# A causal convolution followed by a two-layer product with quick GELU: taps and block sums of the convolution on ScalarE and GpSimd in place of VectorE

## The chip, the cores and the metric

The kernel runs on one core of a Trainium2 chip. A core has TensorE (matmuls, PE in the profile, with PEld for its weight loads), VectorE (DVE), ScalarE (ACT), GpSimd (POOL) and SyncE (SP), which here issues transfers. Each works through its own queue in order, and semaphores tie them together. The metric is the device time of one execution in microseconds (us), the median of the runs.

## The reference, cut to what matters

```python
# x: (8, 4096, 192), weight: (8, 7), w_in: (192, 2048), w_out: (2048, 192)
w = softmax(weight, axis=-1)                 # 8 heads of 24 channels, 7 taps each
x_pad = concatenate([zeros((B, 6, D)), x], axis=1)
y[b, s, h, g] = sum_k w[h, k] * x_pad[b, s + k, h, g]
h = y.reshape(B * S, D) @ w_in
g = h * (1.0 / (1.0 + exp(-1.702 * h)))
return g @ w_out                             # (32768, 192), float32
```

So every token is a weighted sum of itself and the six tokens before it, channel by channel; then come a product to 2048 features, a gating function and a product back to 192 channels. All of it is float32.

## The kernel before, in words

**Tiling.** The 32768 tokens are worked off in 32 steps (`big`) of 1024 tokens: two batches `n` of 512, each as two tiles `o` of 256. The 192 channels are NC = 3 chunks of 64. A convolved chunk lies with both tiles over 128 partitions (64 channels of one tile, 64 of the other) and two blocks of 256 columns (the two batches), so one operation of the convolution has the shape 128 x 512.

**Fewer products.** Both products use a scheme of the Strassen kind. For the first one the six convolved blocks C11 to C32 are joined into V1 to V8 by eight sums (`SUMS_C`, lines 145 to 154), and each of 21 terms (`TERMS`) is one block or sum times one block or sum of `w_in`. For the second, blocks of the gated features are subtracted from one another (`sum_1` to `sum_4`, line 512) and multiplied by blocks of `w_out`.

**A step.** `hidden` (line 531) runs twice in a step, v = 0 and v = 1, with 21 terms each on TensorE (line 492). Four PSUM tiles of two banks, `x`, `y`, `z` and `sums`, are filled, emptied by ScalarE (copies to k15, k16, k18, k19, k20 at lines 543, 549, 557, 559, 565; gating at line 509) or joined by VectorE (lines 554, 562, 566, 574, 575, 587), and filled again. Then `output` (line 649) runs five rounds of the second product (line 597, with line 614), adds their parts (lines 671 to 708), transposes them (line 632) and stores them.

**The preparation of a later step.** `prepare(big)` (line 466) yields small pieces of work for step `big`: three transposes of input (line 414), the taps of the convolution (`conv`, lines 424 to 433), the eight sums (`sums_c`, line 435) and the transfers that bring blocks across the two halves of the partitions (`cross`, line 438). A tap is one operation on VectorE: tap 0 multiplies (line 429), taps 1 to 6 multiply and add to what is there (line 431). The chunks go in the order 0, 2, then the first sum V1 with its transfer, then chunk 1 and the other seven sums.

**What sets the order.** The schedule is written by hand: instructions stand in each engine's queue in the order in which the program makes them. `work(us)` (line 716) takes pieces from the list `todo` as long as their noted cost fits into the given allowance (0.76 for a tap, 0.48 for tap 0, 0.38 for a sum, 0.7 for a transpose); `need(label)` takes all up to a label. The pieces for step `big + 2` are put on the list when the hidden passes of `big` are done, and are taken at the `work` calls in `output` of `big` and in the two `hidden` passes of `big + 1`:

```python
gelu(B11, 0, v, x)                                   # v = 0 and 1
...
act.copy(k16, sums)
last()
if v:
    work(3.2)
pe(y, 6, 14, first=True)
vec.tensor_sub(x, z, k15)
work(2.6)
pe(sums, 13)
act.copy(k19, sums)
```

Further calls are `work(1.1)` after line 566, `work(2.3)` before line 574, and `work(1.2)` and `work(0.7)` around the last two terms. In `output` they are 3.0, 0.7, 0.7 and 4.0. In the queue of the engine that does it, a piece stands exactly where its `work` call is. Buffers bind as well: TensorE may write a PSUM tile again only when ScalarE or VectorE has read it, and k16 shares its memory with u1 and u2 of `output`.

The first step (`first_step`) prepares its own blocks on several engines, and `prepare(1)` runs within it.

Of the kernel before, what the change touches and what calls it, by code (L numbers as in the profile page):

```python
# [8 lines left out]
F32 = mybir.dt.float32  # L9
# [6 lines left out]
def kernel(  # L16
# [29 lines left out]
    nc = tc.nc  # L46
# [5 lines left out]
    P = 128  # L52
# [5 lines left out]
    T = 256  # L58
# [17 lines left out]
    consts = ctx.enter_context(tc.tile_pool(name="consts", bufs=1))  # L76
# [6 lines left out]
    vec, act = nc.vector, nc.scalar  # L83
# [44 lines left out]
    def half(b, u, cols, small):  # L128
# [16 lines left out]
    SUMS_C = [  # L145
        (V1, C31, "-", C11),
        (V2, V1, "-", C32),
        (V3, C12, "+", V2),
        (V4, C22, "+", V2),
        (V5, C21, "-", V4),  # L150
        (V6, C11, "-", V5),
        (V7, C22, "-", C21),
        (V8, C32, "-", C22),
    ]

    def place(big, b):

        if b == V1:
            return V8 if big % 2 else C31
        return C31 if b == V8 and big % 2 else b  # L160

    def own(big):
        return conv_t[:, big % 2 * 2, :, :]
# [169 lines left out]
        dst = w_in_s[:, NC * i : NC * (i + 1), :]  # L333
        round_piece(i, [(lambda v: v.rearrange("p (k f) -> p k f", k=NC), dst)])

    def add_up(v, dst, a, op, b):
        if op == "+":
            vec.tensor_add(v(dst), v(a), v(b))
        elif op == "-":
            vec.tensor_sub(v(dst), v(a), v(b))  # L340
        elif op == "n":
            vec.scalar_tensor_tensor(
                out=v(dst), in0=v(a), scalar=-1.0, in1=v(b), op0=ALU.mult, op1=ALU.subtract
            )
        else:
            vec.tensor_scalar_mul(v(dst), v(a), -1.0)

    def sums_w_in(i):
        add_up(lambda j: w_in_s[:, j, :], *SUMS_W[i])
# [60 lines left out]
    def transpose_x(big, c, n=None):  # L410
# [7 lines left out]
        if c == NC - 1 and n is None:  # L418
            xins.pop(big)

    def conv_src(big, c, k, ns=slice(0, 2)):
        return xts[big][:, c, ns, Q - PAD + k : Q - PAD + k + T]

    def conv(big, c, k, ns=slice(0, 2)):
        src = conv_src(big, c, k, ns)
        dst = own(big)[:, 2 * c + ns.start : 2 * c + ns.stop, :]
        tap = cw[:, c, k : k + 1]
        if k == 0:
            vec.tensor_scalar_mul(dst, src, tap)
        else:  # L430
            vec.scalar_tensor_tensor(  # L431
                out=dst, in0=src, scalar=tap, in1=dst, op0=ALU.mult, op1=ALU.add
            )

    def sums_c(big, i):
        add_up(lambda j: own(big)[:, place(big, j), :], *SUMS_C[i])

    def cross(big, b0, b1):
        for o in range(2):
# [26 lines left out]
    def prepare(big):  # L466

        for c in range(NC):
            yield "", 0.7, lambda c=c: transpose_x(big, c)
        if big + 1 < N_BIG:  # L470
            yield "", 0.0, lambda: load_x(big + 1)

        v1 = place(big, V1)
        for c in (0, 2):
            for k in range(K):
                yield "", 0.76 if k else 0.48, lambda c=c, k=k: conv(big, c, k)
        yield "", 0.38, lambda: sums_c(big, 0)
        yield f"first {big}", 0.0, lambda: cross_when(True, big, v1, v1 + 1)
        for k in range(K):
            yield "", 0.76 if k else 0.48, lambda k=k: conv(big, 1, k)  # L480
        yield "", 0.0, lambda: cross_when(False, big, 0, C31)
        for i in range(1, len(SUMS_C)):
            yield "", 0.38, lambda i=i: sums_c(big, i)
        rest = (C31, V8) if big % 2 else (C31 + 1, NB)
        yield f"all {big}", 0.0, lambda: cross_when(False, big, *rest)
# [235 lines left out]
    def need(label):  # L721
# [9 lines left out]
        op=ALU.mult,  # L731
# [20 lines left out]
    def first_step(fetch):  # L752
# [6 lines left out]
        for k in range(5):  # L759
            conv(0, 0, k, first)  # L760
# [174 lines left out]
```

## Time and profile before

| | before |
|---|---|
| time, median of 2 runs | 2352.9 us (2352.79 to 2353.01) |
| span of the profiled execution | 2351.6 us |
| mean granted TensorE clock | 0.999 |
| ScalarE's gating from SBUF (line 509) | 310 of 1058 ns |
| ScalarE's gating from PSUM (line 509) | 167 of 1016 ns and 35 of 1022 ns |
| VectorE's subtractions of gated blocks, 128 x 2048 (line 512) | 124 of 2284, 62 of 2292, 62 of 2262 ns |
| GpSimd | 23 instructions, 5.8 us busy |
| crossing transfers of V1 (64 KB each) | 1.9 us to landing |

A busy share is an average over the span; whether an engine holds up another is read from the waits and from the order of time. In a group's row the columns are the line, engine, operation, tiles written and read with their shapes, the count, then busy time and the mean ns of one, then the engine's idle time before these operations and who ended it. In a list of waits a row says which engine waited at which line for whom: total us, times, longest.

### The profile page before, as it was taken

How to read it: one execution, taken by the hardware profiler on the slowest of the kernel's cores; microseconds unless marked ns; L12 is line 12 of the kernel's file. 1: busy time of each engine (PE TensorE's matmuls, PEld its weight loads, DVE VectorE, ACT ScalarE, POOL GpSimd, SP SyncE). 2: the span in 40 equal slices, each digit the busy share in tenths (PEclk: the TensorE clock that was granted, in tenths of full speed). 3: DMA queues.
4: the chain of work that ended last, by engine and by line, in shares of the span. 5: the costliest groups of instructions: out<-in, count | busy, mean ns of one | idle time of the engine just before them, and what ended most of it. 6: DMA issues, size and time to landing. Idle time of an engine off the chain costs nothing.

```text
span 2351.6 us, 39193 instructions
## 1 busy us (share of the span) xinstructions
PE 2343.7 (100%) x16856; PEld 892.0 (38%) x16856; DVE 1951.7 (83%) x2186; ACT 1018.4 (43%) x1159; POOL 5.8 (0%) x23
## 2 busy tenths in 40 slices
PE   9999999999999999999999999999999999999998
PEld 5533333333333333333333333333333333333333
DVE  8988888888888888888888888888888888888866
ACT  7234543345533355433454334543345533345433
POOL 0000000000000000000000000000000000000000
PEclk9999999999999999999999999999999999999999
DMA  8323313323123232132331332312323223231010
GB/s 182 69 48 76 68 21 64 63 57 68 36 49 66 55 69 50 35 65 55 68 64 22 68 64 58 68 30 54 67 55 69 46 39 67 55 68 43 17 41 15
DMA packets 197484, 133.67 MB, mean 57 GB/s; under 512 B 108592, under 2 KB 187824, under 8 KB 193344
## 3 DMA queue, kind: packets, MB, share of 16 engines
q1 hardware_dynamic: 196448, 130.92, 27.5%
q8 instruction: 132, 2.16, 0.4%
q14 instruction: 40, 0.33, 0.0%
q10 hardware_dynamic: 832, 0.20, 0.0%
q0 software_dynamic: 32, 0.07, 0.0%
HBM read 53.15 MB, written 25.17 MB: 33 GB/s over the span
## 4 chain that ended last, share of the span: by engine, by line
PE 67%; issue 32%; DMA 0%; DVE 0%; POOL 0%; POOLq 0%; DVEq 0%
PE slot L492 24%; PE slot L597 22%; PE sums L492 11%; PE sums L597 9%; PE slot L614 1%; PE slot L740 0%; PE sums L390 0%; DMA conv_t<-conv_t 0%; DVE xt L414 0%; PE slot L401 0%; POOLq L930 0%; POOL xin L94 0%; PE slot L390 0%; POOL osbs masks.py:199 0%; POOL osbs masks.py:197 0%
## 5 line engine op out<-in xcount | busy, mean ns | idle before, releaser
L492 PE MATMUL slot<-conv_t,w_in_s 64*128 64x512 f32 x3740 | 851.8, 590 | 0.0
L597 PE MATMUL slot<-g,w_out_s 128*32 128x512 f32 (+2 forms) x6864 | 788.7, 568 | 0.0
L492 PEld LDWEIGHTS slot<-conv_t,w_in_s 64*128 64x128 f32 x3740 | 359.6, 187 | 446.8 <-issue 394.6
L431 DVE SCALAR_TENSOR_TENSOR conv_t<-xt,cw,conv_t 128x512 f32<-128x512 f32 (+1 forms) x576 | 424.8, 738 | 13.0
L597 PEld LDWEIGHTS slot<-g,w_out_s 128*32 128x32 f32 x6864 | 241.8, 110 | 455.9 <-issue 439.0
L492 PE MATMUL sums<-conv_t,w_in_s 64*128 64x512 f32 x1660 | 405.4, 592 | 0.0
L509 ACT ACTIVATE g<-room 128x1024 f32<-128x1024 f32 x310 | 321.1, 1058 | 97.5 <-DVE room L574 58.3
L597 PE MATMUL sums<-g,w_out_s 128*32 128x512 f32 (+1 forms) x2304 | 335.0, 587 | 0.0
L512 DVE TENSOR_TENSOR g<-g 128x2048 f32<-128x2048 f32 (+1 forms) x126 | 283.2, 2267 | 4.7 <-PE sums L597 2.4
L492 PEld LDWEIGHTS sums<-conv_t,w_in_s 64*128 64x128 f32 x1660 | 158.3, 187 | 202.9 <-issue 160.9
L509 ACT ACTIVATE g<-slot 128x1024 f32<-128x1024 f32 x167 | 169.4, 1016 | 88.7 <-PE slot L492 88.7
L597 PEld LDWEIGHTS sums<-g,w_out_s 128*32 128x32 f32 x2304 | 93.1, 110 | 152.7 <-issue 146.3
L512 DVE TENSOR_TENSOR room<-g 128x2048 f32<-128x2048 f32 (+1 forms) x64 | 144.6, 2259 | 4.3
L512 DVE TENSOR_TENSOR g<-room,g 128x2048 f32<-128x2048 f32 (+1 forms) x64 | 140.2, 2229 | 0.0
L685 ACT COPY osbs<-slot 32x512 f32<-32x512 f32 (+1 forms) x32 | 18.3, 572 | 251.6 <-PE slot L614 251.6
L597 PE MATMUL slot<-room,w_out_s 128*32 128x512 f32 (+1 forms) x816 | 112.9, 567 | 0.0
L597 PE MATMUL sums<-room,w_out_s 128*32 128x512 f32 x768 | 112.7, 592 | 0.0
L686 DVE TENSOR_TENSOR room<-room,slot 96x512 f32<-96x512 f32 (+1 forms) x32 | 21.6, 675 | 91.1 <-ACT osbs L685 91.1
L670 ACT COPY osbs<-slot 32x512 f32<-32x512 f32 (+1 forms) x32 | 18.4, 574 | 174.4 <-PE slot L597 174.4
L554 DVE TENSOR_TENSOR slot<-slot,room 128x1024 f32<-128x1024 f32 x62 | 75.4, 1216 | 10.8 <-ACT g L509 10.8
L566 DVE TENSOR_TENSOR room<-slot,room 128x1024 f32<-128x1024 f32 x62 | 75.9, 1225 | 6.8 <-DVE room L562 0.5
L574 DVE TENSOR_TENSOR room<-room,sums 128x1024 f32<-128x1024 f32 x31 | 37.8, 1221 | 48.4 <-PE sums L492 48.4
(151 smaller groups left out, 1522.1 us busy)
## 6 DMA issues: line engine op xcount, KB each, us to landing
xin<-in_x_dram SPq DMA_DIRECT2D x240, 180.0 KB, 5.6
conv_t<-conv_t SPq DMA_DIRECT2D x62, 512.0 KB, 4.5
out_dram<-osbs SPq DMA_DIRECT2D x180, 128.0 KB, 2.5
conv_t<-conv_t SPq DMA_DIRECT2D x62, 256.0 KB, 3.6
conv_t<-conv_t SPq DMA_DIRECT2D x62, 64.0 KB, 1.9
xin<-in_x_dram SPq DMA_DIRECT2D x16, 160.0 KB, 5.5
osbs<-in_moe_w_out_dram SPq DMA_DIRECT2D x2, 768.0 KB, 8.8
out_dram<-osbs SPq DMA_DIRECT2D x20, 64.0 KB, 1.8
```

The costliest lines, as they stand in the source:

```text
L431: vec.scalar_tensor_tensor(out=dst, in0=src, scalar=tap, in1=dst, op0=ALU.mult, op1=ALU.add)
L492: nc.tensor.matmul(slot[:, h, :], w_in_s[halves[h], a, v * P : (v + 1) * P], src, start=first, stop=True, skip_group_check=True,)
L509: act.activation(g[:, b, u, v, :, :], src, AF.Gelu_apprx_sigmoid)
L512: vec.tensor_sub(*(half(x, u, cols, small) for x in (dst, a, b)))
L554: vec.tensor_sub(x, z, k15)
L566: vec.tensor_sub(k19, z, k19)
L574: vec.tensor_add(k20, k20, sums)
L597: nc.tensor.matmul(dst[l * Q : (l + 1) * Q, :], w_out_s[:, a, j, c * Q : (c + 1) * Q], half(b, u, cols, small)[:, v, h, :], start=(first a ...
L614: nc.tensor.matmul(dst[l], w_out_s[:, a, j, c * Q : (c + 1) * Q], half(b, u, cols, small)[:, v, h, :], start=(i == 0), stop=(i == NK // 4 ...
L670: act.copy(chunk(v3, 1), blocks(p3c))
L685: act.copy(chunk(v4, 0), blocks(p4c))
L686: vec.tensor_add(v1, v2, p5)
```

## The change

From step 2 on the convolution leaves VectorE. Tap 0 is a multiplication on ScalarE straight into the block. Each of the taps 1 to 6 becomes two operations: ScalarE multiplies into one of six scratch tiles (`taps`, used in turn), and GpSimd adds the scratch to the block. The eight sums of blocks become additions and subtractions on GpSimd. Steps 0 and 1 are as before. Its purpose is to take load off VectorE and give it to the two engines that have less to do. The `work` calls and the noted costs of the pieces stay as they are.

```diff
-    def add_up(v, dst, a, op, b):
+    def add_up(v, dst, a, op, b, eng=vec):
         if op == "+":
-            vec.tensor_add(v(dst), v(a), v(b))
+            eng.tensor_add(v(dst), v(a), v(b))
         elif op == "-":
-            vec.tensor_sub(v(dst), v(a), v(b))
+            eng.tensor_sub(v(dst), v(a), v(b))
...
+    NT = 6
+    taps = consts.tile([P, NT, 2, T], F32)
+    turn_of = [0]
...
         tap = cw[:, c, k : k + 1]
-        if k == 0:
+        if big > 1:
+            if k == 0:
+                act.mul(dst, src, tap)
+                return
+            tmp = taps[:, turn_of[0] % NT, :, :]
+            turn_of[0] += 1
+            act.mul(tmp, src, tap)
+            nc.gpsimd.tensor_add(dst, dst, tmp)
+        elif k == 0:
             vec.tensor_scalar_mul(dst, src, tap)
         else:
             vec.scalar_tensor_tensor(
...
     def sums_c(big, i):
-        add_up(lambda j: own(big)[:, place(big, j), :], *SUMS_C[i])
+        add_up(
+            lambda j: own(big)[:, place(big, j), :],
+            *SUMS_C[i],
+            eng=nc.gpsimd if big > 1 else vec,
+        )
```

## The prediction

> **What bounds the kernel now.** I read the page's busy line first, then the chain of work that ended last, then the list of waits, and last the order of ScalarE's work in one steady step.
>
> ```profile
> PE 2343.7 (100%) x16856; PEld 892.0 (38%) x16856; DVE 1951.7 (83%) x2186; ACT 1018.4 (43%) x1159; POOL 5.8 (0%) x23
> ...
> PE 67%; issue 32%; DMA 0%; DVE 0%; POOL 0%; POOLq 0%; DVEq 0%
> ```
>
> A busy PE need not be a PE at its rate, so I checked the rate. The chain in order of time has runs of 64 matmuls of L597 in 6.87 us (0.1073 each) and of 36 of L492 in 7.72 us (0.2144 each). Multiplied by the counts: 5400 x 0.2144 = 1158; 10352 matmuls of 512 columns on L597 and L614 x 0.1073 = 1111; 784 of 256 columns at half of that = 42; 128 of 128 columns about 4; L740 10.4. Sum 2325 us. Of the 2351.6 us span only 27 us (1.1%) isn't TensorE at its steady rate. VectorE's 83% stands beside this and not on it, and the chain has 0% DVE.
>
> The waits show how near ScalarE is:
>
> ```profile
> PEld sums L492 <- ACT room L549: 13.1, 31, 0.8
> ...
> PEld slot L492 <- ACT g L509: 7.9, 32, 0.6
> ...
> PEld slot L492 <- ACT room L557: 7.3, 31, 0.2
> ...
> PEld slot L492 <- ACT room L543: 4.5, 16, 0.3
> ```
>
> In nearly every step TensorE comes to these PSUM tiles just as ScalarE has emptied them. Waits of 0.1 to 0.4 us are still swallowed by the matmuls in flight; there is little beyond that. Here is ScalarE in a steady step (start, duration, work, idle before):
>
> ```profile
> 611.46 1.01 ACT L549 COPY room<-slot 128x1024 f32<-128x1024 f32 x1 [0.99 <-DVE osbs L632]
> 613.73 1.01 ACT L557 COPY room<-slot 128x1024 f32<-128x1024 f32 x1 [1.26 <-PE slot L492]
> ...
> 618.09 1.01 ACT L565 COPY room<-slot 128x1024 f32<-128x1024 f32 x1
> 618.98 2.02 ACT L509 ACTIVATE g<-room 128x1024 f32<-128x1024 f32 x2
> 621.92 1.06 ACT L509 ACTIVATE g<-room 128x1024 f32<-128x1024 f32 x1 [0.93 <-DVE room L574]
> 622.89 1.00 ACT L509 ACTIVATE g<-slot 128x1024 f32<-128x1024 f32 x1
> 623.79 1.02 ACT L582 COPY sums<-slot 128x1024 f32<-128x1024 f32 x1
> 624.73 1.05 ACT L509 ACTIVATE g<-room 128x1024 f32<-128x1024 f32 x1
> 626.66 1.01 ACT L543 COPY room<-sums 128x1024 f32<-128x1024 f32 x1 [0.88 <-PE sums L492]
> ...
> 631.76 1.01 ACT L557 COPY room<-sums 128x1024 f32<-128x1024 f32 x1 [0.55 <-PE sums L492]
> ```
>
> The 43% is an average. In the two hidden passes of this step (606.55 to 642.6 us, 42 terms of 4 matmuls, 0.858 us each) ScalarE has 26 operations at about 0.95 us from start to start: 24.7 of 36.0 us. It rests in the output products that follow.
>
> **What the Trainium skill says.** *ScalarE: Activation LUTs*, "What ACT_TABLE_LOAD costs": an ACTIVATE with one pointer operand takes 280 ns + 0.833 ns per element, and neighbours overlap by 93 ns; for 512 that is 707 ns, 614 from start to start. The trace agrees (below). *GPSIMD Engine Reference*, section 3.1: a float32 two-input add of 2048 elements takes 4497 ns on GpSimd, 1.96 times VectorE's. The trace has only one of 64 elements. *SBUF — State Buffer*, "SBUF: two separate sides": GpSimd and VectorE share a port pair as an exclusive lock, against VectorE operations with two SBUF inputs or in a two-port mode; the loser waits for the whole instruction. No row of before shows this, since GpSimd does nothing then.
>
> **The change part by part.** The rows that price it:
>
> ```profile
> L431 DVE SCALAR_TENSOR_TENSOR conv_t<-xt,cw,conv_t 128x512 f32<-128x512 f32 x558 | 416.1, 746 | 12.4
> L340 DVE TENSOR_TENSOR conv_t<-conv_t 128x256 f32<-128x256 f32 x186 | 73.2, 421 | 3.2
> L429 DVE TENSOR_SCALAR conv_t<-xt,cw 128x512 f32<-128x512 f32 x93 | 43.6, 468 | 0.0
> L734 ACT ACTIVATE g<-room,cw 128x64 f32<-128x64 f32 x7 | 1.8, 334 | 0.8 <-DVE cw L408 0.8
> L274 POOL TENSOR_TENSOR room<-osbs 128x64 f32<-128x64 f32 x1 | 0.3, 307 | 0.0
> ```
>
> *Removed from VectorE*, per step: 18 x 0.746 + 3 x 0.468 + 8 x 0.42 = 18.2 us of its 60 us. It was hidden behind TensorE, so worth nothing by itself. One thing is returned: in the first pass L549 waits for L632, the last turn of VectorE's output work, because k16 and u1, u2 are one buffer. With no taps ahead of it that turn ends about 0.9 us sooner, and L549 starts when TensorE's term ends, at 611.2 and not 611.46.
>
> *Added to GpSimd*: between 307 ns at 64 and 4497 at 2048 lie 2.11 ns per element, so an add of 512 is estimated at 1.25 us, a sum of 256 at 0.71; 18 x 1.25 + 8 x 0.71 = 28.2 us of a 72.45 us step (the same run of matmuls returns every second step, at 570.43 and 715.31 us in the chain). Who waits for it: the crossing DMA of V1, and ScalarE when it reuses one of six scratch tiles. V1 comes out about 19 us into the hidden passes and is wanted by TensorE after 32; the other sums end about 37 us in and are wanted at 72. The longest run of scratch writes is 4, and each add six back is done by then. All hidden. Lock: VectorE's L512 work (8 x 2.28 = 18.2 us a step) stands in the output part, where only two adds of GpSimd fall; the subtractions are wanted 1.9 us or more after they end, so one add of 1.25 us is hidden.
>
> *Added to ScalarE*: 21 multiplications a step. L734 shows 7 of 64 elements in 1.78 us: 0.332 us each, 0.24 from start to start. L309 (768 elements, pointer bias) takes 0.936 and its kind starts 0.84 apart. Linear between: at 512, 0.72 us, and 0.62 from start to start. That is 13.0 us a step, 8.1 of it (13 of 21) in the hidden passes: 24.7 + 8.1 = 32.8 of 36.0. They fit on average, but the queue is in order and `work` puts them in bunches ahead of operations that empty PSUM. The order of the changed program shows: 3 ahead of L557, 1 ahead of the two gelus at 618.98 and 3 behind them, 2 ahead of L543 of the second pass, 4 ahead of its L557. The other 8 lie in the output part, where ScalarE is idle for 4 to 8 us at a time: nothing. On the trace's times:
>
> 1. First L557: L549 at 611.20, free at 612.12, three multiplications to 613.98, copy done at 614.99. TensorE wants it at term 10, 615.13. Holds by 0.14: 0.
> 2. L565 at 618.09, free 618.99; one multiplication, two gelus (619.61, 620.57), three multiplications from 621.53; gelu of k20 at 623.39 and of x at 624.36, done at 625.37. The second pass begins by writing that slot at 606.55 + 21 x 0.858 = 624.57. With 0.08 us from ScalarE's end to TensorE: **0.9 us**.
> 3. Copy at 625.26, gelu at 626.20, two multiplications from 627.16, L543 at 628.40, done 629.41. TensorE, already 0.9 late, has done its term and x's two by 628.88 and must add to that tile: **0.6 us**.
> 4. L549 at 630.71 and last pass's gelu at 631.61, four multiplications from 632.57, L557 at 635.06, done 636.07. TensorE is at that tile by 634.64: **1.5 us**.
>
> After that the step has no multiplications up to the output part, and ScalarE catches up. Sum 3.0 us a step; blocks 2 to 31 are made this way, in 30 steps: 90 us. 2352.9 + 90 = 2443.
>
> Ends: without any overlap of neighbours (0.72) the nine multiplications of items 2 to 4 add 0.9 us and item 1 gives about 0.2: 4.1 a step, 2476. If each of the three waits is 0.3 us shorter (matmuls in flight swallow as much in the waits above): 2.1 a step, 2416.
>
> **The rivals.** *ScalarE's slack hides it, no change.* For it: 43% busy, 3.2 us left in the hidden passes by the sum above. Then 2353, and since only 27 us aren't TensorE at its rate, 2326 is the floor, so faster by 2% (2306) is out. Against: the bunches stand where the waits list shows the least room. Part of it, under 1.5 us a step, ends below 2400. Chance 0.14.
> *GpSimd or its lock adds to it, slower still.* For it: adds of 512 aren't in the trace. Against: 28.2 us and VectorE's 19.6 us with two SBUF inputs leave 25 us of the step; adds would have to take over 2.3 us to fill it. If the lock also held VectorE's PSUM reads (L554, L562, L574), one add's 1.25 us would fall on the path in each step: 30 x 4.25 = 128, 2480. With adds at 3 us, GpSimd's 67 us and VectorE's 19.6 exceed the step by 14 us: 2352.9 + 30 x 14 = over 2770. Chances 0.16 and 0.04.
> *ScalarE's bunches delay TensorE*, the forecast: 0.66, near 2443.
>
> **How the numbers follow.** Below 2400 lies the first rival (0.14, of which 0.01 is faster by 2%, kept for an error in the rate); above 2490 some of the second and its extreme (0.08). Between are 0.78. 2% is 2400, so slower by over 2% has 0.85, within 2% 0.14.
>
> **What would show it.** Right: waits of TensorE for L509, L543's and L557's lines of about 1.0, 0.6 and 1.5 us, each some 30 times; steps of 75.5 us; VectorE near 60%, ScalarE near 60%, GpSimd near 36%; the chain passing through ScalarE. Wrong: TensorE still without waits; ScalarE idle waiting for GpSimd (ring of scratch); VectorE's operations stretched beside adds; or an add far from 1.25 us.

## The result and the profile after

The changed kernel takes 2444.5 us (2443.61 to 2445.39) against 2352.9 us: ratio 1.0388, interval 1.0358 to 1.0418. It is slower by 92 us, as forecast (2443, range 2400 to 2490).

The busy line and the chain of the page after:

```profile
PE 2372.2 (97%) x16856; PEld 884.5 (36%) x16856; DVE 1475.5 (60%) x1316; ACT 1397.5 (57%) x1789; POOL 1015.3 (42%) x803
...
PE 76%; ACT 17%; issue 5%; POOL 0%; DMA 0%; SPq 0%; DVE 0%; ACTq 0%; POOLq 0%; DVEq 0%
```

VectorE is relieved by 476 us, and the time goes up. ScalarE, which had no share of the chain, now holds 17% of it. GpSimd, busy for 42%, holds none. TensorE's waits tell where (lines of the changed kernel: L559 copies to k15, L573 to k19, L525 is the gelu):

```profile
PE slot L508 <- ACT room L573: 19.6, 16, 3.0
PE sums L508 <- ACT room L573: 19.4, 15, 3.0
PE slot L508 <- ACT g L525: 15.1, 30, 0.5
PE slot L508 <- ACT room L559: 3.8, 15, 0.3
PE sums L508 <- ACT room L559: 3.8, 15, 0.3
```

Three kinds of wait, some 30 times each. No row of this list has TensorE waiting for VectorE or, after the first microseconds, for GpSimd. Now a steady step in order of time, TensorE first. The page counts a wait only after the modelled end of the matmuls before it, so I measure from the start of one run of matmuls, plus 0.858 us for each of its terms (4 matmuls), to the start of the next.

```profile
648.16 3.60 PE L508 MATMUL slot<-conv_t,w_in_s 64*128 64x512 f32 x16
652.26 1.13 PE L508 MATMUL slot<-conv_t,w_in_s 64*128 64x512 f32 x4 [0.50 <-ACT g L525]
653.22 1.08 PE L508 MATMUL sums<-conv_t,w_in_s 64*128 64x512 f32 x4
654.14 1.88 PE L508 MATMUL slot<-conv_t,w_in_s 64*128 64x512 f32 x8
656.27 1.13 PE L508 MATMUL sums<-conv_t,w_in_s 64*128 64x512 f32 x4 [0.25 <-ACT room L559]
657.23 1.88 PE L508 MATMUL slot<-conv_t,w_in_s 64*128 64x512 f32 x8
658.95 1.02 PE L508 MATMUL sums<-conv_t,w_in_s 64*128 64x512 f32 x4
659.81 1.88 PE L508 MATMUL slot<-conv_t,w_in_s 64*128 64x512 f32 x8
662.86 1.99 PE L508 MATMUL sums<-conv_t,w_in_s 64*128 64x512 f32 x8 [1.17 <-ACT room L573]
664.68 0.59 PE L508 MATMUL slot<-conv_t,w_in_s 64*128 64x512 f32 x2
```

Four terms from 648.16 end at 651.59 and the next starts at 652.26: 0.67 us. Two terms from 654.14 end at 655.86, the next starts at 656.27: 0.41. Two from 659.81 end at 661.53, the next starts at 662.86: 1.33. The runs behind a wait are each stretched by about 0.1 us (652.26 to 653.22 is 0.96 and not 0.86). Together 2.8 us. ScalarE in the same stretch:

```profile
648.41 1.33 ACT L438 ACTIVATE taps<-xt,cw 128x512 f32<-128x512 f32 x2
649.64 0.71 ACT L434 ACTIVATE conv_t<-xt,cw 128x512 f32<-128x512 f32 x1
650.25 1.04 ACT L525 ACTIVATE g<-room 128x1024 f32<-128x1024 f32 x1
651.20 1.01 ACT L525 ACTIVATE g<-slot 128x1024 f32<-128x1024 f32 x1
...
654.00 1.33 ACT L438 ACTIVATE taps<-xt,cw 128x512 f32<-128x512 f32 x2
655.22 1.00 ACT L559 COPY room<-sums 128x1024 f32<-128x1024 f32 x1
...
659.37 2.55 ACT L438 ACTIVATE taps<-xt,cw 128x512 f32<-128x512 f32 x4
661.82 0.99 ACT L573 COPY room<-sums 128x1024 f32<-128x1024 f32 x1
```

The gelu of x ends at 652.21 and TensorE starts at 652.26; the copy to k15 ends at 656.22, TensorE starts at 656.27; the copy to k19 ends at 662.81, TensorE starts at 662.86. Each time a row of multiplications stands ahead of what TensorE waits for: right ahead of the two copies, and one gelu further ahead of the gelu of x. From its first multiplication to that operation ScalarE had no pause.

Over 26 steps, from the run of matmuls at 296.41 to that at 2252.47 us, a step takes 75.23 us; before, 16 steps from 280.68 to 1440.20 give 72.47. That is 2.76 us a step. The steps 1 and 2 lose more: the run that follows the hidden passes of step 1 starts at 141.96 and not 135.56 us (6.4 us), and of the 9.3 us that steps 2 and 3 lose together, 6.8 are step 2's (it lasts from 141.96 to 221.18, and before from 135.56 to 208.00). 6.4 + 9.3 + 27 x 2.76 = 90.2; the profiled spans differ by 90.3.

### The profile page after: what moved, and what is told of

Its sections match the earlier page's. It is cut to its first block, busy times and chain, and to the rows that moved or that the text cites. A ratio compares the mean times of both kernels' runs of the same rounds, so it can differ in the third digit from the quotient of the medians.

```text
span 2441.9 us, 40464 instructions
## 1 busy us (share of the span) xinstructions
PE 2372.2 (97%) x16856; PEld 884.5 (36%) x16856; DVE 1475.5 (60%) x1316; ACT 1397.5 (57%) x1789; POOL 1015.3 (42%) x803
## 4 chain that ended last, share of the span: by engine, by line
PE 76%; ACT 17%; issue 5%; POOL 0%; DMA 0%; SPq 0%; DVE 0%; ACTq 0%; POOLq 0%; DVEq 0%
PE slot L613 30%; PE slot L508 21%; PE sums L613 13%; PE sums L508 11%; ACT g L525 7%; ACT taps L438 5%; PE slot L630 2%; ACT room L573 1%; ACT room L559 1%; ACT room L581 1%; ACT sums L598 1%; ACT slot L598 1%; ACT conv_t L434 0%; DMA osbs<-in_moe_w_in_dram 0%; POOL conv_t L439 0%
## 5 line engine op out<-in xcount | busy, mean ns | idle before, releaser
L439 POOL TENSOR_TENSOR conv_t<-conv_t,taps 128x512 f32<-128x512 f32 x540 | 824.9, 1528 | 1285.2 <-ACT taps L438 1261.4
L508 PE MATMUL slot<-conv_t,w_in_s 64*128 64x512 f32 x3740 | 868.5, 595 | 38.5 <-ACT room L573 19.6
L508 PEld LDWEIGHTS slot<-conv_t,w_in_s 64*128 64x128 f32 x3740 | 354.4, 187 | 509.8 <-issue 381.5
L508 PE MATMUL sums<-conv_t,w_in_s 64*128 64x512 f32 x1660 | 410.5, 598 | 23.2 <-ACT room L573 19.4
L525 ACT ACTIVATE g<-room 128x1024 f32<-128x1024 f32 x310 | 320.2, 1055 | 67.3 <-DVE room L603 38.4
L438 ACT ACTIVATE taps<-xt,cw 128x512 f32<-128x512 f32 x540 | 356.0, 714 | 1.4
L525 ACT ACTIVATE g<-slot 128x1024 f32<-128x1024 f32 x167 | 169.6, 1018 | 61.5 <-PE slot L508 61.5
L528 DVE TENSOR_TENSOR room<-g 128x2048 f32<-128x2048 f32 (+1 forms) x64 | 172.8, 2700 | 4.3
L701 ACT COPY osbs<-slot 32x512 f32<-32x512 f32 (+1 forms) x32 | 18.3, 572 | 230.7 <-PE slot L630 230.7
L340 POOL TENSOR_TENSOR conv_t<-conv_t 128x256 f32<-128x256 f32 x180 | 140.0, 791 | 7.1
L578 DVE TENSOR_TENSOR room<-sums,room 128x1024 f32<-128x1024 f32 x31 | 38.0, 1225 | 119.4 <-ACT room L573 119.4
L578 DVE TENSOR_TENSOR room<-slot,room 128x1024 f32<-128x1024 f32 x31 | 38.0, 1225 | 117.5 <-ACT room L573 117.5
```

The source lines that it names most:

```text
L340: eng.tensor_sub(v(dst), v(a), v(b))
L438: act.mul(tmp, src, tap)
L439: nc.gpsimd.tensor_add(dst, dst, tmp)
L508: nc.tensor.matmul(slot[:, h, :], w_in_s[halves[h], a, v * P : (v + 1) * P], src, start=first, stop=True, skip_group_check=True,)
L525: act.activation(g[:, b, u, v, :, :], src, AF.Gelu_apprx_sigmoid)
L528: vec.tensor_sub(*(half(x, u, cols, small) for x in (dst, a, b)))
```

## The experiments

Two theories stood against each other. *Position*: ScalarE's multiplications cost only where they stand ahead of an operation on whose PSUM tile TensorE is about to wait. The rivals: *GpSimd or the port that it shares with VectorE* costs it, or *ScalarE's load as such* does.

**ScalarE's part alone.** The kernel before, with the multiplications beside it:

```diff
         tap = cw[:, c, k : k + 1]
+        if big > 1:
+            act.mul(taps[:, turn_of[0] % 6, :, :], src, tap)
+            turn_of[0] += 1
```

> The kernel before, with all its work on VectorE, and beside it ScalarE makes the 21 products of a step into scratch that nobody reads, at the same places in its queue. GpSimd does nothing. ScalarE theory (its bunches ahead of PSUM copies make TensorE wait): the whole loss is here, 2440 to 2455, a little over the changed kernel because the last turn of the output work is late again (first L557 copy 0.2 to 0.3 us late each step). GpSimd or port-lock theory: 2353, at most 2360.

2447.3 us, ratio 1.0397 (1.038 to 1.0415). The products are read by nobody, GpSimd is idle and VectorE as loaded as before (80% of a longer span), and the loss is the whole of it. A step takes 75.38 us (748.65 less 597.89, halved), 0.15 us over the changed kernel's. The late turn shows there: the 24 matmuls behind the copy to k16 take 5.29 us from start to start (640.12 to 645.41) and 5.15 in the changed kernel (639.57 to 644.72). TensorE's longest waits are the same three:

```profile
PE slot L498 <- ACT room L563: 20.0, 16, 3.0
PE sums L498 <- ACT room L563: 19.5, 15, 3.0
PE slot L498 <- ACT g L515: 15.1, 30, 0.5
```

**GpSimd's part alone.** VectorE makes the products, GpSimd adds:

```diff
-                act.mul(dst, src, tap)
+                vec.tensor_scalar_mul(dst, src, tap)
...
-            act.mul(tmp, src, tap)
+            vec.tensor_scalar_mul(tmp, src, tap)
```

> The changed kernel, but VectorE makes the products (into the same scratch, tap 0 into the block) and GpSimd adds them and makes the sums. ScalarE is left as in the kernel before. ScalarE theory: 2353, between 2343 and 2358, since TensorE waits for neither VectorE nor GpSimd; a few us below 2353 are possible because VectorE's queue is shorter. GpSimd or port-lock theory: the loss stays, 2400 or more.

2356.4 us, ratio 1.0014 (1.0007 to 1.0021). So with GpSimd doing all its adds the loss is 3 us and not 92. Where these 3 come from is seen in VectorE's order of time: its own products, some 0.4 us each in the first row below, take two to three times as long beside GpSimd's adds. In the changed kernel VectorE makes no such products.

```profile
606.21 1.63 DVE L438 TENSOR_SCALAR taps<-xt,cw 128x512 f32<-128x512 f32 x4
607.76 1.49 DVE L434 TENSOR_SCALAR conv_t<-xt,cw 128x512 f32<-128x512 f32 x1
...
627.65 3.96 DVE L438 TENSOR_SCALAR taps<-xt,cw 128x512 f32<-128x512 f32 x4
```

The turns behind them end later, and the copy to k16 (L565 here) with them, for which TensorE was just in time before: the 24 matmuls behind it take 5.22 us from start to start (614.21 to 619.43) and not 5.15. That is 0.07 us in each of 30 steps. In step 1 TensorE also waits for VectorE, once and for 0.6 us (L590), and that step is 0.9 us longer.

**The sums alone on GpSimd.** The taps stay on VectorE:

```diff
-        add_up(lambda j: own(big)[:, place(big, j), :], *SUMS_C[i])
+        e = nc.gpsimd if big > 1 else vec
+        add_up(lambda j: own(big)[:, place(big, j), :], *SUMS_C[i], eng=e)
```

> The kernel before with only the eight sums of a step on GpSimd; taps stay on VectorE. ScalarE theory: 2353 within 2 us. Port-lock theory for the small loss with adds on GpSimd (2356 where VectorE made the products): with 8 operations of 0.72 us in place of 26 the loss is under 1 us. If the sums' longer way to the crossing transfer mattered: over 2358.

2353.0 us, ratio 1.0 (0.9992 to 1.0008): no difference, as expected.

**The same work, one bunch moved.** In the second pass, with the changed kernel otherwise as it is:

```diff
-        if v:
-            work(3.2)
         pe(y, 6, 14, first=True)
         vec.tensor_sub(x, z, k15)
-        work(2.6)
+        if not v:
+            work(2.6)
...
         act.copy(k20, x)
+        if v:
+            work(3.2)
+            work(2.6)
```

> The changed kernel with the same operations, but in the second hidden pass the pieces of work(3.2) and work(2.6) are taken behind the copy to k20 and not ahead of the copy to k19. Position theory (a bunch costs only where it stands ahead of a copy that TensorE needs): the third wait of each step goes (1.33 us and 0.1 us of slower matmuls, in 28 steps 40 us), and in steps 1 and 2 the waits of 3.0 us with the slow matmuls after them (4.8 us each): 2395, between 2388 and 2402; step 72.44 + 1.36 = 73.8 us. Theory of ScalarE's load as such (57% busy, or 13 more operations in 36 us): no change, 2444.

2406.0 us, ratio 1.0226 (1.0211 to 1.0241): 38 us less with not one operation less. A step takes 73.79 us (26 steps from 297.59 to 2216.11), where 73.8 was expected. The total missed by 11 us and lies above the expected band; the reason stands in step 1 alone:

```profile
PE slot L508 <- POOL conv_t L439: 9.6, 1, 9.6
```

In step 1 the moved bunch held the second half of chunk 2's taps; the sum V1 was ready only at 141.3 us, and its crossing transfer came after that. TensorE stood still from 134.2 to 144.0 us, and the twelve matmuls after that took 5.49 us where 2.74 is the rule: 12 us. (The row names the add that ended last before 144.0; it is V1 that TensorE needs.) Here GpSimd's chain was on the path, once in the run.

**Every product made twice**, the second into scratch that nobody reads:

```diff
             act.mul(tmp, src, tap)
+            act.mul(extra[:, turn_of[0] % 2, :, :], src, tap)
```

> The changed kernel with each product of taps 1 to 6 made twice by ScalarE, the second time into scratch that nobody reads (18 more operations a step, 11 of them in the hidden passes). ScalarE theory, by the same sum as in the prediction: first copy to k19 late by 1.6 us more, the gelu before the second pass by 1.9, the copy to k15 by 1.2, the second copy to k19 by 2.5; that last wait passes 3 us, and the matmuls after it run slowly for another 1.6 us as after the waits of steps 1 and 2: 8.8 us a step more, about 2444 + 265 = 2710, between 2670 and 2750. GpSimd or port-lock theory: 2444 to 2460.

2742.6 us, ratio 1.166 (1.1643 to 1.1678), in the expected band and above its middle. A step takes 85.33 us, 10.1 more than the changed kernel's, for 8.8 by the sum. The longest wait passes 3 us as expected, but what follows it costs more than the 1.6 us taken for it:

```profile
901.68 1.88 PE L510 MATMUL slot<-conv_t,w_in_s 64*128 64x512 f32 x8
907.19 3.79 PE L510 MATMUL sums<-conv_t,w_in_s 64*128 64x512 f32 x8 [3.63 <-ACT room L575]
910.76 2.87 PE L510 MATMUL slot<-conv_t,w_in_s 64*128 64x512 f32 x8
913.47 1.88 PE L510 MATMUL sums<-conv_t,w_in_s 64*128 64x512 f32 x8
```

TensorE's gaps at the first copy to k19, the gelu, the copy to k15 and the second copy to k19 measure 1.7, 2.5, 1.7 and 3.8 us in a step, against 0, 0.7, 0.4 and 1.3 in the changed kernel: 7.3 us more, where the expectation had 7.2. The rest is slow matmuls: after a gap of 3.8 us (903.40 to 907.19) eight matmuls take 3.79 us and the next eight 2.87, where 1.88 is the rule: 2.9 us.

**All of it where ScalarE rests.** Pieces are taken in the output part as far as they fit, three multiplications ahead of the first copy to k19, four behind the second pass's copy to k20:

```diff
-        work(4.5 if small else 0.7)
+        work(4.5 if small else 2.2)
...
-        work(0.7)
+        work(0.7 if small else 2.2)
...
-        work(1.5 if small else 4.0)
+        work(1.5 if small else 5.1)
```

In the passes of steps from 2 on, `work(1.1)`, `work(2.3)`, `work(1.2)` and `work(0.7)` are called for v = 1 only, and `work(3.2)` and `work(2.6)` of v = 1 stand behind `act.copy(k20, x)`. Block 2 stays on VectorE.

> The change's division of work, with its products placed where ScalarE rests: in steps from 2 on, of the 21 products of a step 14 stand in the output part, 3 in the first hidden pass ahead of the copy to k19 (the place that cost nothing in the changed kernel), 4 in the second pass behind the copy to k20, none elsewhere in the passes. Block 2 stays on VectorE as in the kernel before. Position theory: no wait of TensorE of 0.2 us or more in a steady step, step 72.2 to 72.6 us, time 2353 within 6 us either way. Not faster by more than 10 us, since VectorE isn't on the path: a steady step of before has only about 0.35 us that isn't TensorE at its rate. Theory of load as such (ScalarE's 57%, GpSimd and its lock in the output part, where the two-input subtractions are): 2380 or more, with TensorE waiting for VectorE's subtractions or ScalarE for the ring of scratch.

2356.7 us, ratio 1.0013 (1.0006 to 1.0019). ScalarE is as busy as in the changed kernel (1390 against 1398 us), GpSimd more (56%), and the loss is gone. A steady step takes 72.44 us (24 steps from 429.48 to 2168.02), the kernel before's. The 3 us that remain lie in the first steps: from 135.57 to 284.61 us two steps take 3.9 us more than before's, and the only wait in TensorE's own list after the start is one of 2.4 us, put down to GpSimd:

```profile
PE slot L508 <- POOL conv_t L439: 2.4, 1, 2.4
```

It is V1 again, in step 2: its sum on GpSimd ends at 205.1 us and TensorE, which stopped at 205.27, goes on at 207.80. The 12 matmuls after it lose another 1.7 us. So GpSimd's chain can come onto the path, where V1's taps are taken late.

No version beat the kernel before. A step has 168 matmuls at 0.2144 us and 336 at 0.1073, 72.07 of its 72.44 us, so with VectorE off the path none of these could by more than some 10 us.

## Why the prediction was right, point by point

**The bound.** 27 us of the span not at TensorE's rate meant that relief of VectorE could bring next to nothing. In the arrangement with the products where ScalarE rests, VectorE is 410 us less busy (1541 against 1952) and the step is no shorter: 72.44 against 72.47. Shown.

**ScalarE's prices.** 0.72 us and 0.62 from start to start were read off shapes of 64 and 768 elements. The rows after have 714 ns, and four in a row take 2.55 us, (2.55 - 0.71) / 3 = 0.61. The price worked out from *ScalarE: Activation LUTs*, "What ACT_TABLE_LOAD costs" (707 and 614 ns), agrees.

**The three waits.** They came at the operations named, in the order named. Their sizes were 0.67, 0.41 and 1.33 where 0.9, 0.6 and 1.5 were worked out, and about 0.1 us of stretched matmuls behind each: 2.76 a step for 3.0. That the first copy to k19 would hold was right: it has no wait in a steady step.

**The count of steps.** Here the sum was wrong in a term that the total hides. All 30 steps were given the same bunches. In steps 1 and 2 the list of pieces was still fuller, and seven multiplications (one into the block, six into scratch) stood ahead of the second copy to k19, not four. ScalarE and then TensorE in step 2:

```profile
204.43 0.71 ACT L434 ACTIVATE conv_t<-xt,cw 128x512 f32<-128x512 f32 x1
205.05 3.77 ACT L438 ACTIVATE taps<-xt,cw 128x512 f32<-128x512 f32 x6
208.72 0.99 ACT L573 COPY room<-sums 128x1024 f32<-128x1024 f32 x1
```

```profile
204.88 1.88 PE L508 MATMUL slot<-conv_t,w_in_s 64*128 64x512 f32 x8
209.77 3.39 PE L508 MATMUL sums<-conv_t,w_in_s 64*128 64x512 f32 x8 [3.01 <-ACT room L573]
212.94 2.23 PE L508 MATMUL slot<-conv_t,w_in_s 64*128 64x512 f32 x8
```

Those two steps cost 6.4 and 6.8 us where 3.0 each stood in the sum, 7 us more; the other 28 cost 0.25 us less each, 7 us less. The two errors cancel, and the nearness of 2443 to 2444.5 is luck to that extent.

Two slips in the working are small. Items 2 to 4 list 1 + 3, 2 and 4 multiplications, which are ten and not nine; the upper end would be 0.1 us a step higher. And if 0.14 lies below 2400 with 0.01 of it faster by 2%, 0.13 is left within 2%, and not 0.14.

**GpSimd.** An add was put at 1.25 us and takes 1.27 alone; a sum at 0.71 and takes 0.72. The busy share came out at 42% and not 36%: an add takes 1528 ns on average, and the rows below show an add's time containing its wait for the port. That lock, which *SBUF — State Buffer* describes in "SBUF: two separate sides", is seen in the changed kernel: GpSimd first, then VectorE.

```profile
607.00 2.00 POOL L439 TENSOR_TENSOR conv_t<-conv_t,taps 128x512 f32<-128x512 f32 x1 [11.53 <-ACT taps L438]
619.62 5.37 POOL L439 TENSOR_TENSOR conv_t<-conv_t,taps 128x512 f32<-128x512 f32 x1 [10.62 <-ACT taps L438]
```

```profile
607.89 3.25 DVE L528 TENSOR_TENSOR room<-g 128x2048 f32<-128x2048 f32 x1
619.36 4.48 DVE L528 TENSOR_TENSOR g<-g 128x2048 f32<-128x2048 f32 x2
```

The first add waits for the end of a subtraction, and the next subtraction then waits for the add: 3.25 us and not 2.29. The second add finds two subtractions one behind the other and ends only 1.15 us after the second of them (623.84 to 624.99). VectorE's operations with one input in PSUM aren't stretched beside adds: the subtraction into k15 takes 1225 ns for 1220 before, the addition into k20 1221 in both. So the rival that let the lock hold for them is out. The prediction had named VectorE operations stretched beside adds as a sign of being wrong. The sign came (the subtractions into `room` take 2747 ns on average and not 2292), but none of it reached TensorE: only two adds fall beside the subtractions, and their results are wanted later.

**The ring of scratch.** No row has ScalarE waiting for GpSimd. Six tiles were enough.

## What to carry to other kernels

An engine that is 43% busy has no room where the engine that bounds the kernel is just about to need it: ask of every operation that is moved to a queue what stands behind it there and who waits for that, not how much time the engine has in sum. Here the same 21 multiplications a step cost 2.8 us, 1.3 us or nothing, by their place in ScalarE's order alone. Work taken off an engine that wasn't on the path brought nothing here, so it could be moved only to where it costs nothing.

## What the runs showed of the hardware that wasn't expected

A long wait of TensorE can cost more than itself. After gaps of 3.17 us (206.60 to 209.77 above) and 3.8 us (903.40 to 907.19, with doubled products) the matmuls lost another 1.9 and 2.9 us. The trace shows why: the granted clock of TensorE is 0.50 from 210.50 to 213.50 and from 907.19 to 910.76, and 1.00 ahead of both gaps. After gaps up to 1.35 us the matmuls behind lost only 0.1 to 0.2.

Between these lengths the runs differ. With doubled products a gap of 2.5 us comes in almost every step, and the matmuls after it lose 0.1 to 0.2 us (380.74 to 382.00: clock 1.00). In the last experiment one gap of 2.53 us (205.27 to 207.80) was followed by a clock of 0.50 (208 to 210) and a loss of 1.7 us. So the length of a gap alone doesn't decide; what else does isn't shown. *TensorE: Matmul & The Clock Gate*, Part 1, names a clock gate that halves the rate after an idle window of about 3.4 us. The halved clock agrees; here gaps shorter than that were followed by it too. So in a kernel like this one a wait that nears 2.5 us is worth cutting first.
